# Gated linear attention into a gated layer on one core: late units form queries and decayed states over all partitions and move them, in a new order

## The chip, the cores and the metric

One core of one Trainium2 chip runs the kernel. The metric is device time in microseconds (us) of one execution. Five engines work side by side and wait for each other through semaphores: PE (TensorE, matrix products), DVE (VectorE), ACT (ScalarE), POOL (GpSimd) and SP (SyncE, which here issues nearly all transfers, one after the other in the order of its queue).

## The reference

Inputs are q, k, v and alpha of shape (4, 8, 768, 48), that is 4 sequences, 8 heads, 768 steps, 48 features, and three weight matrices. First a linear attention with a decay for each feature:

```
for t in range(S):
    state = alpha[:, :, t, :, None] * state + einsum('bhd,bhe->bhde', k[:, :, t], v[:, :, t])
    y[:, :, t] = einsum('bhd,bhde->bhe', q[:, :, t], state)
```

Then y, as x of shape (3072, 384), goes through a gated layer with d_ff = 1536:

```
gate = 1 / (1 + exp(-(x @ w_gate)))
out  = (gate * (x @ w_val)) @ w_out
```

The weights come in as 64-bit floats.

## The kernel before

**The layer.** The 3072 tokens are six groups of 512. The 1536 columns of d_ff are twelve pieces of 128, so there are 72 steps (L712 on). A step computes gate and value of one piece for one group: nine matmuls of 512 columns each (L237), three for each of three products, since x and the weights are each split into a high and a low part and high*high, high*low and low*high are added. ACT makes the sigmoid `sg`, DVE multiplies (L727), ACT rounds the product to `hh` (L728), DVE makes the rest `hl` (L729), and nine matmuls (L737) add hh and hl times w_out into three banks `po`. A step is 27 matmuls of 512 columns.

**The weights.** In the first pass over the twelve pieces, each piece is loaded in halves into one of a few `raw` buffers (two of their own, others borrowed from the tiles of weights that are not made yet: `first_w`), and turned into high and low words: a cast of the top bits (ACT, L368, or DVE for the halves in CASTS, L366), a shift-and-or on DVE (L371), a copy to the high part on ACT (L374), and a subtraction to the low part on DVE (L381). For the three halves in SUMS, the low part is written as a negative copy by ACT and added up by a transfer of POOL (L378).

**The attention.** Each group has four pairs of heads, so there are 24 units of one group and one pair, numbered 0 to 23. The two heads of a pair stand on partitions 0 to 47 and 64 to 111. A unit is cut into chunks. Scans along time on DVE make the running decay from the chunk's end, `G` (L409), and from its start, `F` (L413); keys are multiplied by G (`kt`, L417), queries by F. PE makes scores and each chunk's addition to the state; DVE masks the scores into `A` and runs the states through the chunks (`st`), a chain of small operations (L674); the states times the decay `dec` are needed with the queries for the part of the output that comes from earlier chunks. `yt` holds the outputs, and SP moves them into the x tiles of the next group (L462), where heads and partitions are laid out anew.

Units 0 to 5 use chunks of 128. Units 6 to 23 are `late` units with chunks of 64. Their output is one matmul for each head and chunk (L693): the 128 partitions of its operands hold the masked scores and v on one half and the query and the decayed state on the other. For head 0 the query lies on partitions 0 to 63 of `A[:, 0]`, for head 1 on 64 to 127 of `A[:, 1]`. So before, SP loads each half of the query straight into `A` (L624), and DVE multiplies each half by F in place, 64 partitions by 512 (L632, two for each unit); POOL multiplies states by `dec` on each half, 64 by 384, into `vs` (L681, two for each unit).

**The order.** Each operation is handed to a planner (`Plan.add`) with its engine, an estimated duration, a due time and what it reads and writes. The planner places all operations by a model of the engines, and among those that are ready takes the one that is due first. SHIFTS moves the due time of single operations, by their number. Each engine then runs its list in that order. PE's list begins with WARM = 29 products of nothing useful while the first unit is made.

Of the kernel before, what the change touches and what calls it, by code (L numbers as in the profile page):

```python
# [198 lines left out]
def act(n):  # L199
    return 0.01 + n / 1065  # L200
# [40 lines left out]
def chunked(ctx, tc, rows, vc, vh, vg, weights_in, out, const, ident, flags, weights, within):  # L241
# [63 lines left out]
    r_F = ring("F", 2, T, early=[borrow("x1", T)])  # L305
    r_G0, r_dec = ring("G0", 2, EH), ring("dec", 4, EH)
# [42 lines left out]
    def weight_piece(f, key):  # L349
        cuts = (0, DM, 2 * DM, WF) if f == 0 else (0, WF // 2, WF)  # L350
        over = before(f"w{f}") if f >= 6 else []
        for i, (lo, hi) in enumerate(zip(cuts, cuts[1:])):
# [22 lines left out]
            if (f, i) in SUMS:  # L375
                plan.add("scalar", act(n), kk, lambda low=low, word=word: nc.scalar.activation(
                    out=low(), in_=word, func=AF.Copy, scale=-1.0), [rl, ("wh", f, i)], [("w", f, i)])
# [228 lines left out]
    def late(u, g, p, t):  # L606
# [3 lines left out]
        plan.add("sync", (0.475, P * A_Q * 4 / RATE), t["load"], lambda: nc.sync.dma_start(  # L610
            out=tin[:, 0:A_Q], in_=rows[g, p, :, 0:A_Q]), writes=[(inn, m) for m in "ark"])
        kT = tin[:, A_K:A_Q]
# [10 lines left out]
        for j in range(2):  # L623
            plan.add("sync", (0.475, R * T * 4 / RATE), t["more"], lambda j=j: nc.sync.dma_start(  # L624
                out=A[own[j], j], in_=rows[g, p, own[j], A_Q:WIDTH]), writes=[(an, 2 + j)])
        plan.add("sync", (0.475, P * CH * 2 * D * 4 / RATE), after(t["more"], 0.1), lambda: nc.sync.dma_start(
            out=v.rearrange("p c j e -> p (c j e)"), in_=vc[g, p]), writes=[(vn, "v")])
        for j in range(2):
            plan.add("sync", (0.475, R * EH * D * 4 / RATE), after(t["more"], 0.2), lambda j=j: nc.sync.dma_start(
                out=vs[other[j], j].rearrange("p c e -> p (c e)"), in_=vh[g, p, j]), writes=[(vsn, j)])  # L630
        for j in range(2):
            plan.add("vector", 0.61, t["q"], lambda j=j: nc.vector.tensor_tensor(  # L632
                out=A[own[j], j], in0=A[own[j], j], in1=F[own[j]], op=ALU.mult), [fn], [(an, 2 + j)], port=True)
# [209 lines left out]
SUMS = ((3, 0), (5, 1), (9, 0))  # L843
# [171 lines left out]
```

## Time and profile before

| | us |
|---|---|
| median of 3 runs (lowest, highest) | 516.16 (515.01, 516.84) |
| the profiled execution | 515.34 |
| its span on the core | 513.6 |
| PE busy | 503.1 |
| DVE busy | 346.9 |
| ACT busy | 172.3 |
| POOL busy | 95.8 |

The profile is of one execution. Times in it count from the first instruction. Busy time of PE overlaps with itself, since a matmul is shown from its start to the end of its pipeline; what PE really needs for one is read from the distance between two starts. An engine that sits idle and bounds nothing costs nothing. The granted clock is 1.00 (of 2.4 GHz) in the stretches shown below.

### The profile page before, as it was taken

Reading aid. Unit: us, or ns where it says so; the run is one execution under the profiler, and the core shown is the slowest. Engines: PE = TensorE matmul, PEld = TensorE weight load, DVE = VectorE, ACT = ScalarE, POOL = GpSimd, SP = SyncE. Lnnn points to the kernel's source line nnn. Section 1 sums busy time; section 2 is a strip of 40 time slices with the busy share of each in tenths; the row PEclk is TensorE's granted clock in tenths of the full one; section 3 lists DMA queues with packets and bytes.
Section 4 is the critical chain, followed back from the end, with each engine's and each line's share of the span. In section 5 each row is a group of like instructions: output and inputs, shape, how many; then the busy total and the mean of one; then the engine's idle time right before and its main releaser. Section 6 shows DMA issues by size and latency. Waiting matters only on the chain.

```text
span 513.6 us, 10505 instructions
## 1 busy us (share of the span) xinstructions
PE 503.1 (98%) x4223; PEld 428.3 (83%) x4223; DVE 346.9 (68%) x660; ACT 172.3 (34%) x329; POOL 95.8 (19%) x112
## 2 busy tenths in 40 slices
PE   8999999999999999999999999999999999999994
PEld 4878878788888888888888888888888888888884
DVE  7899999999767795669569658568666432222222
ACT  2447665663222133222233323222332222312121
POOL 4450203213302320203113123022021010000000
PEclk9999999999999999999999999999999999999999
DMA  8857985760724553624625625435633000100001
GB/s 313 300 145 226 308 266 177 210 201 11 202 40 121 124 115 74 160 56 124 127 45 129 173 60 131 84 87 131 144 88 73 10 8 17 61 1 0 2 1 66
DMA packets 81111, 59.18 MB, mean 115 GB/s; under 512 B 61984, under 2 KB 67360, under 8 KB 81056
## 3 DMA queue, kind: packets, MB, share of 16 engines
q1 hardware_dynamic: 80624, 57.56, 41.4%
q0 software_dynamic: 432, 0.88, 1.0%
q8 instruction: 34, 0.56, 0.5%
q14 instruction: 21, 0.17, 0.1%
HBM read 45.22 MB, written 8.39 MB: 104 GB/s over the span
## 4 chain that ended last, share of the span: by engine, by line
PE 86%; DVE 10%; DMA 1%; issue 1%; ACT 0%; POOL 0%; DVEq 0%; ACTq 0%; POOLq 0%
PE gv L237 49%; PE po L737 26%; PE gv L693 3%; PE at L645 2%; PE gv L704 1%; DVE w L381 1%; PE at L651 1%; DVE raw L371 1%; DMA in<-in_rows_dram 1%; DVE G L409 1%; DVE first_w L371 1%; DVE F L413 1%; PE at L509 1%; DVE hl L729 1%; DVE A L661 1%
## 5 line engine op out<-in xcount | busy, mean ns | idle before, releaser
L237 PE MATMUL gv<-x,w 128*128 128x512 f32 x1296 | 302.2, 380 | 1.1 <-DVE st L537 0.6
L237 PEld LDWEIGHTS gv<-x,w 128*128 128x128 f32 x1296 | 243.7, 189 | 37.9 <-DVE st L537 1.0
L727 DVE TENSOR_TENSOR gv<-gv,sg 128x512 f32<-128x512 f32 x72 | 50.0, 694 | 118.3 <-PE gv L237 117.9
L737 PE MATMUL po<-hh,w 128*128 128x512 f32 x432 | 109.6, 385 | 0.1
L737 PEld LDWEIGHTS po<-hh,w 128*128 128x128 f32 x432 | 79.7, 189 | 12.3 <-ACT hh L728 0.7
L681 POOL TENSOR_TENSOR vs<-st,dec 64x384 f32<-64x384 f32 x36 | 41.8, 1161 | 250.8 <-PE gv L237 177.0
L728 ACT CAST hh<-gv 128x512 fp32r<-128x512 f32 x72 | 42.3, 588 | 126.0 <-DVE gv L727 120.0
L725 ACT ACTIVATE sg<-gv 128x512 f32<-128x512 f32 x72 | 42.9, 596 | 101.0 <-PE gv L237 99.5
L729 DVE TENSOR_TENSOR hl<-gv,hh 128x512 fp32r<-128x512 f32 x72 | 49.6, 689 | 20.8 <-ACT hh L728 18.6
L737 PE MATMUL po<-hl,w 128*128 128x512 f32 x216 | 60.3, 380 | 0.5 <-DVE hl L729 0.5
L737 PEld LDWEIGHTS po<-hl,w 128*128 128x128 f32 x216 | 40.7, 189 | 7.0 <-DVE hl L729 1.3
L674 DVE SCALAR_TENSOR_TENSOR st<-st,dec,at 128x48 f32<-128x48 f32 x144 | 38.0, 264 | 4.3
L409 DVE TENSOR_TENSOR_SCAN G<-in,d1g 128x512 f32<-128x512 f32 x22 | 33.5, 1523 | 3.2 <-DMA in<-in_rows_dram 3.2
L632 DVE TENSOR_TENSOR A<-A,F 64x512 f32<-64x512 f32 x36 | 32.1, 893 | 2.2 <-DMA A<-in_rows_dram 1.7
L661 DVE TENSOR_TENSOR A<-at,mask 64x256 f32<-64x256 f32 x72 | 30.2, 420 | 3.7 <-PE at L651 3.0
L417 POOL TENSOR_TENSOR in<-in,G 128x512 f32<-128x512 f32 x17 | 23.0, 1353 | 28.5 <-PE gv L430 17.2
L413 DVE TENSOR_TENSOR_SCAN F<-in,d1f 128x512 f32<-128x512 f32 x22 | 27.7, 1258 | 0.5
L423 ACT ACTIVATE F<-F 128x512 f32<-128x512 f32 x23 | 14.5, 632 | 21.5 <-DVE A L632 19.9
L693 PE MATMUL gv<-A,vs 128*48 128x64 f32 x576 | 19.8, 221 | 0.0
L693 PEld LDWEIGHTS gv<-A,vs 128*48 128x48 f32 x576 | 17.1, 123 | 2.1 <-POOL vs L681 0.7
L419 ACT COPY starts<-G 128x8 f32<-128x8 f32 (+1 forms) x23 | 4.7, 203 | 33.1 <-DVE G L409 33.1
L645 PEld LDWEIGHTS at<-A,in 48*64 48x64 f32 x576 | 10.2, 134 | 6.6 <-issue 6.0
(137 smaller groups left out, 330.9 us busy)
## 6 DMA issues: line engine op xcount, KB each, us to landing
in<-in_rows_dram SPq DMA_DIRECT2D x18, 516.5 KB, 4.4
raw<-in_w_dram SPq DMA_DIRECT2D x14, 577.0 KB, 4.1
first_w<-in_w_dram SPq DMA_DIRECT2D x8, 577.0 KB, 4.7
A<-in_rows_dram SPq DMA_DIRECT2D x36, 128.0 KB, 3.3
out_dram<-raw SPq DMA_DIRECT2D x18, 256.0 KB, 2.5
v<-in_vc_dram SPq DMA_DIRECT2D x20, 192.0 KB, 3.0
way<-G SPq DMA_DIRECT2D x14, 256.0 KB, 3.2
kn<-way SPq DMA_DIRECT2D x56, 64.0 KB, 4.2
```

What stands on the lines that cost most here:

```text
L237: nc.tensor.matmul(out=dst, lhsT=lhs(a, i), rhs=rhs(b, i), start=(n == 0 and i == 0), stop=(n == len(todo) - 1 and i == NK - 1))
L409: plan.add("vector", scan(n), t["G"], lambda: nc.vector.tensor_tensor_scan(out=G[:, ::-1], data0=az[:, n:0:-1], data1=d1g[size], initial=0 ...
L413: plan.add("vector", scan(n), after(t["G"], 0.01), lambda: nc.vector.tensor_tensor_scan(out=F, data0=az[:, 0:n], data1=d1f, initial=0.0, o ...
L661: plan.add("vector", 0.43, t["mask"], lambda pa=pa, j=j, i=i: nc.vector.tensor_tensor(out=A[other[j], j].rearrange("p (c i t) -> p i c t", ...
L674: nc.vector.scalar_tensor_tensor(out=st[:, c + 1, :], in0=st[:, c, :], scalar=dec[:, c:c + 1], in1=pas[c % 2][1][:, T // 2 + c // 2 * D:T ...
L681: plan.add("gpsimd", pool_(EH * D), t["sd"], lambda j=j: nc.gpsimd.tensor_tensor(out=vs[own[j], j], in0=st[own[j], 0:EH], in1=dec[own[j]]. ...
L693: nc.tensor.matmul(out=py[R * j:R * j + D, cs], lhsT=vs[r, j, c, :], rhs=A[r, j, cs], start=True, stop=True)
L725: plan.add("scalar", act(T), first(0.3), lambda: nc.scalar.activation(out=sg, in_=got["g"][1][:, 0:T], func=AF.Sigmoid), [got["g"][0]], [sgn])
L727: plan.add("vector", vec(T), first(0.4), lambda: nc.vector.tensor_tensor(out=pv, in0=pv, in1=sg, op=ALU.mult), [sgn], [pvn])
L728: plan.add("scalar", act(T), first(0.45), lambda: nc.scalar.copy(out=hh, in_=pv), [pvn], [hhn])
L729: plan.add("vector", vec(T), first(0.5), lambda: nc.vector.tensor_tensor(out=hl, in0=pv, in1=hh, op=ALU.subtract), [pvn, hhn], [hln])
L737: nc.tensor.matmul(out=pso_now[m][1][:, 0:T], lhsT=weights.part("o", b, f)[:, m * P:(m + 1) * P], rhs=halves(h[a]), start=(f == 0 and i == ...
```

## The change

For the late units four things are different, and the order is new.

- Queries: the whole row of a unit, its query included, is loaded in one transfer into `in`. One operation multiplies the query by F over 128 partitions, on DVE for the units in WHOLE and from unit 10 on, and on POOL for unit 6 alone. Two transfers of SP move each head's half into its place in `A`.
- States: one POOL operation over 128 by 384 writes the decayed states into a new ring of two tiles, `sd`; two transfers of SP move each half into `vs`.
- The tables: QUERIES (early units whose query product is on DVE) gains 2 and 5; KEYS has 8 in the place of 7; SUMS and CASTS name other halves, three and three, where CASTS named five.
- SHIFTS is another table, so that the planner lays out every engine's list anew. A scratch space for transfers that POOL issues is set to 8192.

```diff
+    r_sd = ring("sd", 2, EH, D)
...
-        plan.add("sync", (0.475, P * A_Q * 4 / RATE), t["load"], lambda: nc.sync.dma_start(
-            out=tin[:, 0:A_Q], in_=rows[g, p, :, 0:A_Q]), writes=[(inn, m) for m in "ark"])
-        kT = tin[:, A_K:A_Q]
+        plan.add("sync", (0.475, P * WIDTH * 4 / RATE), t["load"], lambda: nc.sync.dma_start(
+            out=tin, in_=rows[g, p]), writes=[(inn, m) for m in "arkq"])
+        kT, qT = tin[:, A_K:A_Q], tin[:, A_Q:WIDTH]
...
-        for j in range(2):
-            plan.add("sync", (0.475, R * T * 4 / RATE), t["more"], lambda j=j: nc.sync.dma_start(
-                out=A[own[j], j], in_=rows[g, p, own[j], A_Q:WIDTH]), writes=[(an, 2 + j)])
...
+        e = "vector" if u in WHOLE or u >= 2 * NP + 2 else "gpsimd"
+        plan.add(e, vec(T) if e == "vector" else pool_(T), t["q"], lambda: getattr(nc, e).tensor_tensor(
+            out=qT, in0=qT, in1=F, op=ALU.mult), [(inn, "r"), fn], [(inn, "q")], port=True)
         for j in range(2):
-            plan.add("vector", 0.61, t["q"], lambda j=j: nc.vector.tensor_tensor(
-                out=A[own[j], j], in0=A[own[j], j], in1=F[own[j]], op=ALU.mult), [fn], [(an, 2 + j)], port=True)
+            plan.add("sync", (0.475, 2 * R * T * 4 / RATE), after(t["q"], 0.3), lambda j=j: nc.sync.dma_start(
+                out=A[own[j], j], in_=qT[own[j]]), [(inn, "q")], writes=[(an, 2 + j)])
...
+        qn, sd = r_sd.next()
+        plan.add("gpsimd", pool_(EH * D), t["sd"], lambda: nc.gpsimd.tensor_tensor(
+            out=sd, in0=st[:, 0:EH], in1=dec.rearrange("p (c o) -> p c o", o=1).broadcast_to([P, EH, D]), op=ALU.mult), [sn, decn], [qn])
         for j in range(2):
-            plan.add("gpsimd", pool_(EH * D), t["sd"], lambda j=j: nc.gpsimd.tensor_tensor(
-                out=vs[own[j], j], in0=st[own[j], 0:EH], in1=dec[own[j]].rearrange("p (c o) -> p c o", o=1).broadcast_to([R, EH, D]), op=ALU.mult),
-                [sn, decn], [(vsn, 2 + j)])
+            plan.add("sync", (0.475, 2 * R * EH * D * 4 / RATE), after(t["sd"], 0.2), lambda j=j: nc.sync.dma_start(
+                out=vs[own[j], j], in_=sd[own[j]]), [qn], [(vsn, 2 + j)])
...
-SUMS = ((3, 0), (5, 1), (9, 0))
-CASTS = ((3, 0), (4, 0), (5, 0), (8, 0), (9, 1))
-QUERIES = (0, 1, 4)
-KEYS = (0, 1, 3, 4, 6, 7)
+SUMS = ((3, 0), (3, 1), (6, 1))
+CASTS = ((0, 2), (7, 0), (11, 1))
+QUERIES = (0, 1, 2, 4, 5)
+WHOLE = (4, 5, 7, 8, 9)
+KEYS = (0, 1, 3, 4, 6, 8)
...
-    nc = _bacc.Bacc("TRN2", target_bir_lowering=False, num_devices=1)
+    nc = _bacc.Bacc("TRN2", target_bir_lowering=False, num_devices=1, dynamic_dma_scratch_size=8192)
```

In the rows of the order that follow, a name's number is that of the tile, and lines of the new kernel stand a few numbers higher (L409 is L411, L522 is L524, L729 is L733, L363 is L364).

DVE before, at the start, around the masks of unit 2 (`first_x_77`) and the first scan of unit 3 (L409 on `first_w_74`):

```order
L522 TENSOR_TENSOR A_88<-gv_122,mask_104 128x512
L522 TENSOR_TENSOR A_88<-at_119,mask_104 128x512
L537 SCALAR_TENSOR_TENSOR st_110<-st_110,dec_99,at_120 128x48
L522 TENSOR_TENSOR first_x_77<-gv_123,mask_104 128x512
L522 TENSOR_TENSOR first_x_77<-gv_122,mask_104 128x512
L409 SCALAR_TENSOR_TENSOR G_92<-first_w_74,d1g_102 128x512
L371 SCALAR_TENSOR_TENSOR raw_82<-raw_82,top_84 128x384
```

And in the new order:

```order
L499 TENSOR_TENSOR first_w_75<-first_w_75,first_x_77 128x512
L524 TENSOR_TENSOR A_88<-gv_124,mask_106 128x512
L524 TENSOR_TENSOR A_88<-at_121,mask_106 128x512
L372 SCALAR_TENSOR_TENSOR raw_82<-raw_82,top_84 128x384
L539 SCALAR_TENSOR_TENSOR st_112<-st_112,dec_101,at_122 128x48
L411 SCALAR_TENSOR_TENSOR G_92<-first_w_74,d1g_104 128x512
L524 TENSOR_TENSOR first_x_77<-gv_125,mask_106 128x512
L524 TENSOR_TENSOR first_x_77<-gv_124,mask_106 128x512
```

The scan of unit 3 stands ahead of unit 2's masks now, and unit 2's query product (L499) is DVE's.

DVE before, around the last `hl` of the first pass (L729, `hl_118`), with unit 10's scans (L409, L413 on `in_78`) and unit 9's second query half (L632):

```order
L674 SCALAR_TENSOR_TENSOR st_108<-st_108,dec_97,at_120 128x48
L409 SCALAR_TENSOR_TENSOR G_91<-in_78,d1g_103 128x512
L727 TENSOR_TENSOR gv_121<-gv_121,sg_113 128x512
L632 TENSOR_TENSOR A_88<-A_88,F_94 64x512
L411 TENSOR_TENSOR G_95<-G_91,tiny 128x8
L412 RECIPROCAL d1f<-G_95 128x8
L729 TENSOR_TENSOR hl_118<-gv_121,hh_116 128x512
L413 SCALAR_TENSOR_TENSOR F_93<-in_78,d1f 128x512
```

And in the new order, where the last `hl` is `hl_120` and `w_1322` the last piece of weights:

```order
L372 SCALAR_TENSOR_TENSOR raw_83<-raw_83,top_84 128x576
L415 SCALAR_TENSOR_TENSOR F_94<-in_79,d1f 128x512
L733 TENSOR_TENSOR hl_119<-gv_123,hh_117 128x512
L383 TENSOR_TENSOR w_1322<-raw_83,w_1322 128x576
L473 TENSOR_TENSOR x_675<-x_675 128x512
L631 TENSOR_TENSOR in_79<-in_79,F_94 128x512
L414 RECIPROCAL d1f<-G_97 128x8
L415 SCALAR_TENSOR_TENSOR F_93<-in_78,d1f 128x512
L731 TENSOR_TENSOR gv_123<-gv_123,sg_115 128x512
L631 TENSOR_TENSOR in_78<-in_78,F_93 128x512
L733 TENSOR_TENSOR hl_120<-gv_123,hh_118 128x512
```

Unit 10's scan F and its query product stand ahead of the last `hl` now; its scan G and the maximum after it (L411 before) are further up the list. The state chain of unit 8 (L674) is also further up.

SP before, from the loads of the weights' pieces 7 and 8 on (`raw` and `first_w_76` from `in_w_dram`):

```order
L363 DMA raw_82<-in_w_dram 128x2308
L363 DMA raw_83<-in_w_dram 128x2308
L363 DMA first_w_76<-in_w_dram 128x2308
L624 DMA A_87<-in_rows_dram 64x512 x2
L462 DMA x_685<-yt_86 48x512
L629 DMA vs_89<-in_vh_dram 64x384 x2
L363 DMA raw_82<-in_w_dram 128x2308
L462 DMA x_685<-yt_86 16x512
L610 DMA in_79<-in_rows_dram 128x1033
```

And in the new order, from piece 8 on:

```order
L686 DMA vs_89<-sd_95 64x384 x2
L464 DMA x_675<-yt_86 48x512
L364 DMA first_w_76<-in_w_dram 128x2308
L364 DMA raw_82<-in_w_dram 128x2308
L628 DMA vs_89<-in_vh_dram 64x384
L634 DMA A_88<-in_79 64x512 x2
L464 DMA x_675<-yt_86 48x512
L364 DMA raw_83<-in_w_dram 128x2308
L628 DMA vs_89<-in_vh_dram 64x384
L634 DMA A_87<-in_78 64x512 x2
L364 DMA first_w_76<-in_w_dram 128x2308
L464 DMA x_675<-yt_86 16x512
```

Unit 6's states (`vs_89<-sd_95`), unit 7's query (`A_88<-in_79`) and unit 8's (`A_87<-in_78`) stand between the loads now, each with its wait; the loads of queries from memory are gone.

## Rows read from the trace of the kernel before

**Rows 1.** The page, busy us of each engine (share of the span) and instructions.

```profile
PE 503.1 (98%) x4223; PEld 428.3 (83%) x4223; DVE 346.9 (68%) x660; ACT 172.3 (34%) x329; POOL 95.8 (19%) x112
```

**Rows 2.** Stretches: length, busy us of each engine (x instructions), granted clock, DMA.

```profile
30.00:40.00 10.00, 9.09 (x99) 7.13 (x99) 9.96 (x20) 5.31 (x11) 3.83 (x5) 1.00 0.58 170
130.00:400.00 270.00, 270.00 (x2452) 234.14 (x2451) 192.71 (x370) 76.99 (x155) 56.20 (x52) 1.00 0.46 107
```

**Rows 3.** PE's waits: us in total, times, longest; first and last of seven.

```profile
PE at L704 <- POOL ident masks.py:199: 1.6, 1, 1.6
...
PE gv L237 <- DVE w L381: 0.2, 1, 0.2
```

**Rows 4.** The chain, in order of time: start, us, what.

```profile
102.36 1.03 PE gv L693 x32
...
122.27 1.94 PE gv L237 x9
...
124.66 1.78 PE po L737 x7
```

**Rows 5.** PE's groups in 26.4:124.65: xcount, busy us, mean ns, idle before.

```profile
L237 PE MATMUL gv<-x,w 128*128 128x512 f32 x234 | 55.2, 384 | 1.1 <-DVE st L537 0.6 <-DVE x L602 0.2 <-DVE w L381 0.2
L737 PE MATMUL po<-hh,w 128*128 128x512 f32 x68 | 18.6, 389 | 0.1
L737 PE MATMUL po<-hl,w 128*128 128x512 f32 x33 | 9.8, 385 | 0.5 <-DVE hl L729 0.5
```

**Rows 6.** DVE's timeline, 101:126: start, us, what [idle before, releaser].

```profile
101.65 0.69 DVE L729 TENSOR_TENSOR hl<-gv,hh 128x512 fp32r<-128x512 f32 x1 [0.65 <-ACT hh L728]
...
119.70 1.77 DVE L409 TENSOR_TENSOR_SCAN G<-in,d1g 128x512 f32<-128x512 f32 x1
...
122.57 1.23 DVE L411 TENSOR_TENSOR G<-G,tiny 128x8 f32<-128x8 f32 x1
123.84 0.20 DVE L412 RECIPROCAL d1f<-G 128x8 f32<-128x8 f32 x1
123.96 0.64 DVE L729 TENSOR_TENSOR hl<-gv,hh 128x512 fp32r<-128x512 f32 x1
```

**Rows 7.** DVE's groups in 20:126, columns as in rows 5.

```profile
L413 DVE TENSOR_TENSOR_SCAN F<-in,d1f 128x512 f32<-128x512 f32 x7 | 8.5, 1214 | 0.0
...
L632 DVE TENSOR_TENSOR A<-A,F 64x512 f32<-64x512 f32 x8 | 5.5, 682 | 0.1
...
L366 DVE CAST top<-first_w 128x576 f16<-128x576 bf16 x2 | 1.1, 532 | 0.0
...
L440 DVE STREAM_TRANSPOSE G<-in 128x512 f32<-128x512 f32 x1 | 0.7, 711 | 0.1
...
L497 DVE TENSOR_TENSOR in<-in,F 128x512 f32<-128x512 f32 x1 | 0.7, 676 | 0.0
```

**Rows 8.** DVE's timeline, 17:22.

```profile
19.93 1.29 DVE L522 TENSOR_TENSOR first_x<-gv,mask 128x512 f32<-128x512 f32 x2 [1.20 <-PE gv L509]
21.14 1.22 DVE L409 TENSOR_TENSOR_SCAN G<-first_w,d1g 128x512 f32<-128x512 f32 x1
```

**Rows 9.** POOL's timeline, 50:126.

```profile
51.29 1.83 POOL L497 TENSOR_TENSOR in<-in,F 128x512 f32<-128x512 f32 x1 [4.69 <-DVE F L413]
...
119.56 2.53 POOL L681 TENSOR_TENSOR vs<-st,dec 64x384 f32<-64x384 f32 x2 [13.32 <-DVE st L674]
122.17 1.62 POOL L417 TENSOR_TENSOR in<-in,G 128x512 f32<-128x512 f32 x1
```

**Rows 10.** DMA issues: xcount, KB each, median us to landing.

```profile
raw<-in_w_dram SPq DMA_DIRECT2D x14, 577.0 KB, 4.1
...
A<-in_rows_dram SPq DMA_DIRECT2D x36, 128.0 KB, 3.3
```

**Rows 11.** DVE's timeline, 57.3:62.

```profile
58.12 1.22 DVE L413 TENSOR_TENSOR_SCAN F<-in,d1f 128x512 f32<-128x512 f32 x1
```

**Rows 12.** PE's timeline, 68:71.

```profile
69.06 0.69 PE L645 MATMUL at<-A,in 48*64 48x64 f32 x32
```

More of the change, by code (lines that the diff above doesn't have):

```diff
@@ L374, in weight_piece @@
             plan.add("scalar", act(n), kk, lambda word=word, high=high: nc.scalar.copy(out=high(), in_=word), [rl], [("wh", f, i), *over])
-            if (f, i) in SUMS:
-                plan.add("scalar", act(n), kk, lambda low=low, word=word: nc.scalar.activation(
-                    out=low(), in_=word, func=AF.Copy, scale=-1.0), [rl, ("wh", f, i)], [("w", f, i)])
+            summed = (f, i) in SUMS
+            plan.add(*(("scalar", act(n)) if summed else ("vector", 0.0)), kk, (lambda low=low, word=word: nc.scalar.activation(
+                out=low(), in_=word, func=AF.Copy, scale=-1.0)) if summed else (lambda: None), [rl, ("wh", f, i)], [("w", f, i)])
+            if summed:
                 plan.add("gpsimd", (0.9, P * n * 8 / RATE), kk, lambda low=low, word=word: nc.gpsimd.dma_start(
@@ L840, in chunked @@
         plan.issue()
-SUMS = ((3, 0), (5, 1), (9, 0))
-CASTS = ((3, 0), (4, 0), (5, 0), (8, 0), (9, 1))
-QUERIES = (0, 1, 4)
-KEYS = (0, 1, 3, 4, 6, 7)
-SHIFTS = ((5, -2), (12, -4), (51, 8), (52, 5), (54, 8), (71, 6), (82, 2), (85, 1), (93, -8), (126, 3), (143, 4), (160, 9), (170, 1), (177, 5), (179, 2), (187, 10), (219, -1), (222, 21), (237, -1), (282, 12), (290, -5), (302, 3), (324, 3), (325, -4), (338, 4), (343, -8), (347, -13), (348, -1), (355, 2), (360, 2), (370, 2), (373, 6), (374, 9), (376, 6), (388, 2), (402, 2), (403, 4), (416, -4), (418, 6), (440, -5), (464, -10), (468, 34), (480, -3), (493, 5), (494, 4), (503, -2), (519, 16), (565, -3), (573, -2), (583, 6), (588, -2), (598, -1), (601, 7), (622, -4), (658, 3), (699, 2), (803, 12), (829, 8), (860, 2), (863, -1))
+SUMS = ((3, 0), (3, 1), (6, 1))
[3 more added lines that the diff above has]
+KEYS = (0, 1, 3, 4, 6, 8)
+SHIFTS = ((5, -4), (55, 31), (64, 7), (67, -19), (68, 42), (82, 27), (92, 38), (96, -7), (101, -35), (103, -10), (109, -40), (110, -17), (115, 44), (123, 13), (124, 5), (126, 31), (131, 36), (158, -45), (161, 523), (166, 51), (169, 301), (173, 97), (191, 87), (193, 58), (202, 39), (213, -82), (215, 69), (219, -2), (244, -75), (245, 53), (269, -15), (271, -35), (283, 59), (287, 66), (294, 21), (306, 730), (312, 47), (323, 16), (325, -158), (335, 32), (338, 61), (345, -3), (346, -15), (347, -14), (348, 19), (351, 123), (357, 275), (360, 541), (361, 921), (369, -5), (377, -31), (382, 199), (384, -24), (392, 142), (400, 30), (401, 9), (421, -125), (433, 122), (450, 220), (451, 451), (452, 33), (457, 74), (462, -48), (464, 6), (471, 141), (472, 5), (476, 270), (487, -9), (499, 62), (501, -70), (504, -78), (505, -64), (513, 29), (523, 159), (528, 113), (533, -33), (535, 76), (536, -12), (540, 128), (541, 2), (544, 66), (547, 21), (567, 33), (579, -27), (581, 82), (598, -26), (601, 71), (604, 172), (605, 196), (611, 17), (621, -110), (629, -45), (632, -45), (643, 95), (656, -43), (682, -23), (684, -18))
 WARM = 29
```

## The prediction

> **What bounds the kernel now.** I read the page first, then the stretches, then PE's waits, then DVE's timeline where those waits lie. PE is busy in 98% of the span [rows 1], so a change of this kind can only win what PE loses. The stretches say where it loses: from 130 us on PE is busy without a gap while DVE works 193 of 270 us; in 30:40 it is DVE that is full, 9.96 of 10 us, and PE that has a hole of 0.9 [rows 2]. PE's waits are seven, 3.8 us together; the largest, 1.6 us, is the start of the kernel, and the other six are for DVE [rows 3]. Gaps understate the loss, since a matmul that starts late hides part of it: nine of 512 columns take 1.94 us in a row, 0.2156 us each [rows 4], though each is shown as 0.38 us long [rows 5]. From the first weight matmul at 26.4 us to 124.65 us PE issued 234 + 68 + 33 = 335 of those [rows 5], 72.2 us of issue. The attention matmuls of the same 98.25 us, each bunch from its start to the next one's (as 1.03 us for the outputs of a late unit, L693 [rows 4]; there are some thirty bunches), make 18.6 us. So 98.25 - 72.2 - 18.6 = 7.4 us are lost there. That is the most that the change can win apart from the 26 us of the start.
>
> The end of this stretch is set by DVE: the last `hl` of the first pass over the weights starts at 123.96 us, lasts 0.64 us, and is read by a matmul that starts at 124.66 [rows 4, 6]. Behind it PE has 382.5 us of gapless work and a tail, which no edit touches. So I ask: when does DVE make its last `hl` of the first pass, and how much of PE's work stands behind it then?
>
> **The change part by part.** Durations are means of DVE's rows in 20:126 [rows 7].
>
> Term 1, DVE's own work ahead of that `hl`. Removed: eight half-height query products (units 6 to 9, 8 x 0.682 = 5.5 us) and three 576-column casts of weights (3 x 0.53 = 1.6). Added: four full-height products (units 7 to 10; unit 6 goes to POOL). No row shows a full-height product of a late unit; the nearest is L497, 0.676, so the other 64 partitions are free: 4 x 0.676 = 2.7. Two query products of units 2 and 5 come from POOL: 1.35. One 384-column cast: at most 0.53, I take 0.4. Unit 10 is drawn ahead of the last `hl` with its F scan (1.21), transposition (0.71) and a product of 8 columns (under 0.2). Removed 7.1, added 6.5: -0.5 us. Without unit 10, whose four instructions are 2.7 us, it would be -3.3; both are kept for the range.
>
> Term 2, a stall that is filled. At 18.7 us DVE stood 1.20 us for the scores of unit 2, and then ran masks and a scan of 1.22 us [rows 8]. The order now has that scan ahead of the masks. The scores are as late as before, but the wait is covered: -1.2 us, as long as PE's scores keep their place, which they do. Bounds: -1.2 to 0.
>
> Term 3, POOL in DVE's way. Between the last weight words and the last `hl`, two DVE instructions are stretched: the scan at 119.70 took 1.77 us instead of 1.22, and the 8-column maximum L411 at 122.57 took 1.23 us where the reciprocal of the same 8 columns takes 0.20 [rows 6]. Both ran beside POOL products of SBUF operands, 119.56 and 122.17 [rows 9]. That is 0.55 + 1.03 = 1.6 us. In the new order unit 10's scan and maximum are earlier and unit 8's decayed states, now one POOL product, are long done. But POOL still multiplies unit 10's keys, now ahead of the last weights, so I put 1.0 back; the halved decay products of units 6 and 7 give perhaps 0.2, my estimate. Term 3: -0.8, bounds -1.9 (nothing is stretched again) to +1.0 (unit 9's keys too meet DVE, and unit 6's query adds to it, 1.83 us on POOL as L497 is there [rows 9]). The Trainium skill (SBUF — State Buffer, section "SBUF: two separate sides") says that the pair of ports which DVE and GpSimd share is an exclusive lock, held for a whole instruction. By that rule the two POOL entries would have stopped two-operand work on DVE for all of their 4.15 us, and with unit 10's keys (1.62) put back the term would be -2.5 and the sum -3.0. The trace does not bear this out to the full: DVE went on with other work beside them and lost the 1.6 above.
>
> Term 4, work left behind. Ahead of its last `hl` PE now issues 225 + 103 = 328 of the 512-column matmuls instead of 335 by the order (nine fewer of the second pass, two more of the first); the attention matmuls ahead of it are the same number. Seven are left for later: 7 x 0.2156 = +1.5 us.
>
> Term 5, DVE's wait of 0.65 us for ACT at 101.65 [rows 6]. ACT gets two more casts and DVE's order there is another; I take half of it as gone: -0.3, bounds -0.65 to +0.65.
>
> What I cost at nothing. The transfers: no row shows a move of a query or of states; the nearest are loads of 128 KB, which land in 3.3 us [rows 10]; I take that for both. They lengthen two chains of each unit. Unit 6: F is done at 59.3 us in the old order [rows 11] and its scores start at 69.06 [rows 12]; POOL 1.8, two issues and 3.3 come to about 6.3, so 3 us of cover are left. Later units have their query made about 1.5 steps (8.7 us) ahead of the scores and their states over two steps ahead of the outputs, and DVE has slack from 130 us on [rows 2]. If the cover were gone, each late unit would cost PE the rest of one transfer. The loads of unit rows carry the same bytes as before, in one instead of three. POOL's halved work is off the path later, and the smaller scratch concerns three POOL transfers only.
>
> Sum: -0.5 - 1.2 - 0.8 + 1.5 - 0.3 = -1.3 us. The profiled execution took 515.34 us (span 513.6), 0.8 under the median of 516.16; taken off the median: 514.9, rounded to the side of the larger cover in terms 1 and 3, 514.8.
>
> **The rivals.** About 0.3%, 1.55 us, can be told from no change.
>
> Full relief: early unit 10 is only taken where DVE would wait, so that term 1 counts -3.3, and term 3 -1.1. Then -3.3 - 1.2 - 1.1 + 1.5 - 0.3 = -4.4, or 511.8. For it: DVE is full to 120 us [rows 2]. Against: PE must then find its other inputs sooner too, and 7.4 us is all there is.
>
> No gain: the last `hl` comes earlier but PE meets a wait elsewhere (the last weight words stand 0.7 us of DVE's queue later in this order than before, counted as in term 1), so only the small waits shift: 516.2, give or take 0.8.
>
> Slower: SP. It issues in order, and now two products per unit stand in its queue with their waits. In 80 to 110 us the load of a weight piece stands behind unit 7's query, the move of unit 6's `yt`, or unit 8's query; the load lands after 4.1 us [rows 10], then ACT casts it, then DVE needs it. Between the release of a buffer and its next use lie about 7 us of DVE's queue; 4.1 go to the load, up to 1.5 to the move of `yt` ahead of it, and the cast takes most of the rest, so that three loads (both halves of piece 9, the first of 11) have about half a us to spare each. If each comes 2 us later, DVE stands still three times for 1.5 us; it decides as soon as the sum is over the 1.3 us above: 4.5 - 1.3, net +3, or 519. For it: buffers are only three. Against: the loads mostly wait for their buffer, not for their turn. The Trainium skill (DMA: Bandwidth & Descriptors, section "Anatomy of one DMA") says that a semaphore wait happens on the issuing sequencer before dispatch, so nothing behind it starts; this is that mechanism.
>
> **How the numbers follow.** My forecast 0.50, own range 513.2 to 516.2: a little under half of it is faster by over 0.3%. Full relief 0.23, no gain 0.14, slower 0.13. Faster: 0.24 + 0.23 = 0.47; within 0.3%: 0.26 + 0.14 = 0.40; slower 0.13. The range leaves out a tenth on either side: 510.8 (most of full relief) to 518.0 (half of the slower case).
>
> **What would show it.** Right: no wait of DVE near 19 us; the last `hl` of the first pass at about 121 to 122.5 us; POOL's decay products 18 and not 36; PE without gaps after 130 us. Wrong: weight words on DVE that wait for ACT casts or loads between 85 and 112 us (the slower rival); a PE wait for a query or states moved by transfer; a last `hl` under 120 us (full relief).

## The result and the profile after

The changed kernel took 520.71 us (median of six runs, 518.68 to 522.07), the kernel before 516.29 beside it (six runs, 514.83 to 517.01). The ratio is 1.0087 [1.0060, 1.0113]: slower by 0.9%, or 4.4 us, where I had forecast 1.4 us faster. The profiled execution took 520.46 us, with a span of 518.7.

The page's first part, busy us of each engine in the changed kernel (before: [rows 1]):

```profile
PE 502.8 (97%) x4223; PEld 427.5 (82%) x4223; DVE 321.2 (62%) x641; ACT 174.7 (34%) x331; POOL 70.2 (14%) x93
```

DVE and POOL are each relieved by 26 us, as the change says, and PE's work is the same. So the 5.1 us of span are waits. Busy time by stretch tells where (length, busy us of PE, PEld, DVE, ACT, POOL with their counts, granted clock, DMA share, GB/s). The kernel before:

```profile
20.00:126.00 106.00, 103.47 (x953) 85.82 (x948) 103.52 (x192) 61.00 (x111) 26.55 (x29) 1.00 0.65 196
126.00:140.00 14.00, 14.00 (x153) 12.12 (x152) 10.36 (x21) 4.24 (x8) 4.00 (x4) 1.00 0.71 176
```

The changed kernel:

```profile
20.00:126.00 106.00, 100.28 (x940) 83.08 (x935) 97.14 (x186) 62.64 (x113) 19.09 (x23) 1.00 0.72 217
126.00:140.00 14.00, 12.93 (x141) 10.34 (x141) 9.52 (x21) 4.24 (x8) 2.33 (x3) 1.00 0.66 161
```

PE is busy for 3.2 us less ahead of 126 us and 1.1 us less behind it; from 140 to 400 us it has no gap in either kernel. Of the 6.4 us by which DVE is less busy in the first stretch nothing reached PE. The waits show what took its place. PE's largest from 20 us on (us in total, times, longest):

```profile
PE po L741 <- ACT hh L732: 3.1, 4, 1.8
PE gv L237 <- ACT sg L729: 1.3, 2, 0.7
PE gv L237 <- ACT yt L457: 1.2, 1, 1.2
```

And DVE's in 20:127, where the kernel before had three waits of 1.2, 0.7 and 0.3 us (the first two are in [rows 6, 8]):

```profile
DVE raw L372 <- ACT top L369: 5.0, 4, 2.0
DVE G L411 <- DMA in<-in_rows_dram: 1.0, 1, 1.0
DVE first_w L372 <- ACT first_w L369: 0.6, 1, 0.6
DVE w L383 <- ACT w L375: 0.3, 1, 0.3
```

PE used to wait for DVE [rows 3]; now it waits for ACT, and DVE does too. ACT's timeline shows why (start, us, what, idle before and its releaser), around 65 and 95 us:

```profile
64.67 0.83 ACT L369 CAST top<-raw 128x576 f16<-128x576 bf16 x1 [1.50 <-DMA raw<-in_w_dram]
65.37 0.57 ACT L457 COPY yt<-gv 128x512 f32<-128x512 f32 x1
...
94.18 0.83 ACT L369 CAST top<-raw 128x576 f16<-128x576 bf16 x1 [1.79 <-DMA raw<-in_w_dram]
94.88 0.57 ACT L436 COPY kn<-gv 128x512 f32<-128x512 f32 x1
95.35 0.59 ACT L732 CAST hh<-gv 128x512 fp32r<-128x512 f32 x1
```

PE at the same two places:

```profile
66.00 0.70 PE L237 MATMUL gv<-x,w 128*128 128x512 f32 x2 [1.22 <-ACT yt L457]
...
95.99 0.48 PE L741 MATMUL po<-hh,w 128*128 128x512 f32 x1 [1.76 <-ACT hh L732]
```

The reader is to see a queue here. A cast of weights waits for its load, and what PE needs next (`yt`, which frees a bank; `hh`) stands behind it in ACT's list and waits too, though its own input is long there: the outputs that `yt` copies were made by 61.7 us, the product that `hh` rounds by 92.3. Late loads alone are not the difference. From 20 to 127 us ACT waited 6.3 us for loads of weights, and about as long, 6.0, in the kernel before, where PE has no wait for ACT at all. The third place is the start of the second pass. DVE, 130 to 135 us:

```profile
130.40 1.73 DVE L663 TENSOR_TENSOR A<-at,mask 64x256 f32<-64x256 f32 x4 [2.45 <-PE at L653]
132.14 2.37 DVE L676 SCALAR_TENSOR_TENSOR st<-st,dec,at 128x48 f32<-128x48 f32 x8
134.42 0.69 DVE L731 TENSOR_TENSOR gv<-gv,sg 128x512 f32<-128x512 f32 x1
```

PE there:

```profile
130.30 2.21 PE L237 MATMUL gv<-x,w 128*128 128x512 f32 x9
133.25 2.21 PE L237 MATMUL gv<-x,w 128*128 128x512 f32 x9 [0.75 <-ACT sg L729]
135.79 1.56 PE L741 MATMUL po<-hh,w 128*128 128x512 f32 x6 [0.33 <-ACT hh L732]
```

The gate of the first piece (130.30) comes behind the gate of the next piece and unit 10's scores, and its product waits on DVE behind four masks and eight states.

Gaps understate what is lost, as before. So I counted for each kernel, at every group of PE's list, its start less the issue time of all that stands ahead of it (0.2156 us for a 512-column matmul [rows 4], the others by their own rows). These are worked out from one profiled execution each and are good to about half a us, since the small matmuls have no one price; the kernels from the third row on are the experiments below:

| lost on PE by, us | 27 | 47 | 62 | 97 | 126.6 | 146 | end |
|---|---|---|---|---|---|---|---|
| before | 5.0 | 8.1 | 8.3 | 11.5 | 12.6 | 12.7 | 16.0 |
| changed | 5.1 | 7.3 | 8.2 | 13.9 | 15.5 | 17.5 | 20.5 |
| both_undone | 5.3 | 7.5 | 8.4 | 12.3 | 15.3 | 17.4 | 20.3 |
| sum_on_vector | 5.2 | 7.7 | 8.2 | 11.5 | 13.0 | 15.0 | 18.0 |
| mended2 | 5.2 | 7.4 | 8.0 | 9.6 | 10.2 | 15.9 | 18.9 |
| mended3 | 5.1 | 7.3 | 8.0 | 10.8 | 11.6 | 13.0 | 16.0 |
| mended3_old_ops | 5.2 | 7.4 | 8.0 | 11.9 | 15.3 | 15.7 | 18.6 |

The change loses 2.5 us more than before from 62 to 97 us, 0.5 to 126.6, and 1.9 at the start of the second pass; at the end it is 4.5.

### The profile page after: what moved, and what is told of

It is laid out like the page before. It is cut to its first block, busy times and chain, and to the rows that moved or that the text cites. A ratio compares the mean times of both kernels' runs of the same rounds, so it can differ in the third digit from the quotient of the medians.

```text
span 518.7 us, 10513 instructions
## 1 busy us (share of the span) xinstructions
PE 502.8 (97%) x4223; PEld 427.5 (82%) x4223; DVE 321.2 (62%) x641; ACT 174.7 (34%) x331; POOL 70.2 (14%) x93
## 2 busy tenths in 40 slices
DMA packets 83991, 67.44 MB, mean 130 GB/s; under 512 B 62560, under 2 KB 70240, under 8 KB 83936
## 4 chain that ended last, share of the span: by engine, by line
PE 75%; DVE 15%; DMA 5%; issue 2%; ACT 1%; SPq 0%; DVEq 0%; ACTq 0%
PE gv L237 45%; PE po L741 24%; DMA first_w<-in_w_dram 3%; PE gv L697 3%; PE at L647 2%; DVE G L411 2%; DVE w L383 2%; DVE raw L372 2%; DVE first_w L372 1%; DMA raw<-in_w_dram 1%; DVE st L676 1%; DVE F L415 1%; PE at L653 1%; DVE gv L731 1%; DVE A L663 1%
## 5 line engine op out<-in xcount | busy, mean ns | idle before, releaser
L729 ACT ACTIVATE sg<-gv 128x512 f32<-128x512 f32 x72 | 43.0, 597 | 128.6 <-PE gv L237 128.6
L733 DVE TENSOR_TENSOR hl<-gv,hh 128x512 fp32r<-128x512 f32 x72 | 49.3, 685 | 21.6 <-ACT hh L732 19.7
L741 PE MATMUL po<-hl,w 128*128 128x512 f32 x216 | 61.8, 382 | 0.2 <-DVE hl L733 0.2
L683 POOL TENSOR_TENSOR sd<-st,dec 128x384 f32<-128x384 f32 x18 | 15.5, 862 | 270.0 <-DVE st L676 224.8
L411 DVE TENSOR_TENSOR_SCAN G<-in,d1g 128x512 f32<-128x512 f32 x22 | 30.4, 1381 | 9.4 <-DMA in<-in_rows_dram 9.4
L415 DVE TENSOR_TENSOR_SCAN F<-in,d1f 128x512 f32<-128x512 f32 x22 | 28.9, 1316 | 0.1
L457 ACT COPY yt<-gv 128x512 f32<-128x512 f32 x20 | 11.7, 585 | 14.3 <-PE gv L697 14.3
L473 DVE TENSOR_TENSOR x<-x 128x512 fp32r<-128x512 f32 x15 | 10.3, 688 | 7.5 <-ACT x L471 7.5
```

Source lines behind the costliest of these rows:

```text
L411: plan.add("vector", scan(n), t["G"], lambda: nc.vector.tensor_tensor_scan(out=G[:, ::-1], data0=az[:, n:0:-1], data1=d1g[size], initial=0 ...
L415: plan.add("vector", scan(n), after(t["G"], 0.01), lambda: nc.vector.tensor_tensor_scan(out=F, data0=az[:, 0:n], data1=d1f, initial=0.0, o ...
L729: plan.add("scalar", act(T), first(0.3), lambda: nc.scalar.activation(out=sg, in_=got["g"][1][:, 0:T], func=AF.Sigmoid), [got["g"][0]], [sgn])
L733: plan.add("vector", vec(T), first(0.5), lambda: nc.vector.tensor_tensor(out=hl, in0=pv, in1=hh, op=ALU.subtract), [pvn, hhn], [hln])
L741: nc.tensor.matmul(out=pso_now[m][1][:, 0:T], lhsT=weights.part("o", b, f)[:, m * P:(m + 1) * P], rhs=halves(h[a]), start=(f == 0 and i == ...
```

## The experiments

Two theories stood against each other. M: the new operations cost the time, by the moves that stand in SP's queue and by their traffic, so that weights land late. O: the operations are harmless or good, and the order that was found anew is the worse one. All kernels were timed in five rounds against the kernel before; intervals are of 95%.

**Operations and order taken apart.** A part of the plan keeps its place in every engine's list when only what it issues is changed. So old operations can stand in the new order and new ones in the old.

both_undone and states_undone, the core of the edit for the states (both_undone does the like for the queries):

```
-   plan.add("gpsimd", ..., nc.gpsimd.tensor_tensor(out=sd, in0=st[:, 0:EH], ...
+   plan.add("gpsimd", ..., [nc.gpsimd.tensor_tensor(out=vs[own[j], j], in0=st[own[j], 0:EH], ...) for j in range(2)]
-   plan.add("sync", ..., nc.sync.dma_start(out=vs[own[j], j], in_=sd[own[j]])
+   plan.add("sync", ..., lambda: None)
```

> The changed kernel in its own new order of instructions on every engine, but with the old operations put back in place: the query halves are loaded from DRAM into A by two loads and multiplied on VectorE where the one product stood, the two state products on GpSimd write vs where the one product stood, and no SBUF-to-SBUF move is left (two more A buffers, since in this order the queries come earlier). Theory M (the moves and their waits in SP's in-order queue, and their traffic, make the weight pieces land late): the late loads go away, 515 to 517 us. Theory O (the order that was found for the new kernel, with its casts, sums and shifts, is the worse one whichever way the operations are done): it stays at 520 to 521 us.

Measured: 519.66 us, 1.0083 [1.0068, 1.0097]. Without one of the new operations, the new order is as slow as the changed kernel. But it is not the same loss. By the table both_undone loses 3.9 us from 62 to 97 us, where the changed kernel loses 5.7, and 3.0 to 126.6, where that loses 1.6; ACT's waits for loads at 64 and 94 us are gone, which is what M had named as its sign. The old operations, longer on DVE and POOL, lose elsewhere what the late loads no longer cost. So equal times do not clear the moves by themselves; mended3 below does.

> The changed kernel with the states times decay alone put back: two products of 64 partitions on GpSimd straight into vs in the place of the one, without their 36 moves; the queries stay as changed. Theory M: half of the moves are gone, so a good part of the 4.4 us: 517 to 519 us. Theory O: 520 to 521 us, or a little more, since GpSimd works longer (about 26 us of it in all).

Measured: 520.83 us, 1.0098 [1.0079, 1.0116]. Half of the moves gone, nothing won.

moves_on_pool issues all 72 moves by `nc.gpsimd.dma_start`:

> The changed kernel with all 72 moves issued from GpSimd's queue in place of SP's, in the same places of the order; the traffic is the same. Theory M in its form of the queue (weight loads stand behind moves that wait for their product): 516 to 518 us. Theory M in its form of the traffic (the moves' bytes share the DMA engines with the weights), and theory O: 520 to 521 us or more, as GpSimd takes about 1 us for each issue.

Measured: 519.56 us, 1.0095 [1.0072, 1.0117]. In its profiled execution the wait at 94 us was gone, but its six runs lay between 517.9 and 522.2 us, no better than the changed kernel's. So to take the moves off SP's queue wins nothing as it stands; what POOL's issuing of them costs instead is not told apart.

The other half of the cross is the old order with the new operations. In the first of these two kernels a late unit's whole row could be loaded while an early unit's outputs still had to read their query in that buffer, so those outputs are computed with another unit's query:

> The kernel before in its own old order, with the new operations put in place: whole query rows are loaded, one product of 128 partitions stands where the second of the two stood, and its two moves follow right there; the same for the states. Theory M: slower than before by about what the change cost, 519 to 521 us. Theory O: 515 to 516.5 us, as before or a little faster, since VectorE works less.

Measured: 528.61 us, 1.0253 [1.0229, 1.0277]; since it computes something else it is not counted for O or M. The second loads the query by itself, when its place in `A` is free:

> The kernel before in its own old order of instructions, with the new operations put where the first of each pair of old ones stood: the query rows are loaded whole at the place of the first A load, the one product of 128 partitions and its two moves stand at the place of the first half product, and the same for the states. Theory O (the new order is the cause, the operations are harmless): 515 to 517 us. Theory M (the operations and their moves cost the time): 519 us or more; of that a wait of TensorE for A<-in or vs<-sd would show the move's own 2 to 3 us behind the product, for which the old order has no room.

Measured: 523.88 us, 1.0203 [1.0161, 1.0246]; four of its six runs lay between 523.3 and 524.1 us, two at 528.6 and 529.7. PE's two largest waits from 20 us on:

```profile
PE gv L705 <- DMA vs<-sd: 5.1, 2, 3.4
PE at L652 <- DMA A<-in: 1.4, 1, 1.4
```

Here M has a point: in a list made for operations without moves there is no room for a move behind the product, and PE waits for it. In those places the new operations don't pay, and a new order was needed. In the changed kernel PE has no wait for a move; there it is only that the new order loses time elsewhere.

**The start of the second pass.** MOVED names parts of the plan that are put ahead of others, with everything else as in the changed kernel:

```
+MOVED = ((643, 655),)        # gate of the second pass's first piece, ahead of the next piece's gate
```

> The changed kernel with one group of nine matmuls put earlier on TensorE alone: the gate of the second pass's first weight piece stands ahead of the gate of the next piece and of unit 10's scores and additions (it stood behind them, at 130.30 us), so VectorE has its product out before the four masks and eight states that held it from 132.14 to 134.42 us. Theory O: the 1.7 us that the new order loses between 130 and 137 us go away, about 519 us where the changed kernel has 520.7 (ratio to before 1.005 to 1.006). Theory M: nothing changes, 520.7 us (1.0087).

Measured: 522.84 us, 1.0146 [1.0123, 1.0168]. The edit made it worse, and the trace says why. PE and DVE of gate_first:

```profile
137.35 2.93 PE L746 MATMUL po<-hh,w 128*128 128x512 f32 x6 [3.28 <-ACT hh L737]
```

```profile
131.96 1.73 DVE L668 TENSOR_TENSOR A<-at,mask 64x256 f32<-64x256 f32 x4 [4.39 <-PE at L658]
133.70 2.37 DVE L681 SCALAR_TENSOR_TENSOR st<-st,dec,at 128x48 f32<-128x48 f32 x8
135.98 0.69 DVE L736 TENSOR_TENSOR gv<-gv,sg 128x512 f32<-128x512 f32 x1
```

I had moved PE's group alone. On DVE the product still stood behind the masks, and the masks now came 1.6 us later because PE's scores did. DVE stood idle until 131.96 us, though ACT had made `sg`, the product's last input, by 129.7, where the idle time ahead of ACT's next instruction begins:

```profile
136.71 0.58 ACT L737 CAST hh<-gv 128x512 fp32r<-128x512 f32 x1 [7.01 <-DVE gv L736]
```

> As gate_first, and the product of gate and value of the piece whose po matmuls waited 0.87 us at 117.46 us stands ahead of a transpose and a shift on VectorE, and its hh ahead of two copies on ScalarE. Theory O: another 1.0 us less, about 518 us (ratio 1.003 to 1.004). Theory M: 520.7 us (1.0087).

Measured: 523.05 us, 1.0136 [1.0114, 1.0159]; the same loss hides what the added edit does.

> gate_first with what it lacked: not TensorE's gate group alone goes ahead of unit 10's scores, but also its product on VectorE goes ahead of unit 10's four masks and eight states (in gate_first the product stood behind them in the in-order queue, and TensorE waited 3.28 us for hh). Theory O (the places of a few instructions in the new order): the loss between 127 and 137 us falls from 1.8 us in the changed kernel to about 0.1, so 1.7 us less than the changed kernel, about 519 us where it has 520.7 (ratio to before 1.005 to 1.006). Theory M (the operations and their moves): 520.7 us (1.0087).

Measured: 522.05 us, 1.0139 [1.0121, 1.0157]. PE no longer waits for `hh`, but 2.64 us for `hl`, which stands behind a scan on DVE that waits for rows. My expectation failed a second time, for the same reason one instruction further on.

**The load that comes late.** The row of POOL's timeline that issues the accumulating transfer for piece 3, its landing among the DMA issues (xcount, KB, us to landing), and SP's next load into that buffer, in the changed kernel:

```profile
48.75 0.86 POOL L380 DMA_DIRECT2D w<-raw  x1 [4.59 <-DVE d1f L414]
```

```profile
w<-raw POOLq DMA_DIRECT2D x1, 288.0 KB, 9.3
```

```profile
58.10 0.33 SPq L364 DMA_DIRECT2D raw<-in_w_dram  x1
```

The transfer holds its `raw` from 48.75 to 58.08 us, and the next load starts at 58.10: it is the load for which ACT waits at 64.67. Before, SUMS named (5, 1) and (9, 0) where it now names (3, 1) and (6, 1). gate_product_sum and sum_on_vector make that low part on DVE (the later runs name such halves in ON_VECTOR):

```
-   plan.add("gpsimd", ..., nc.gpsimd.dma_start(out=low().bitcast(F32), in_=word, accum_op=ALU.add), ...)
+   plan.add("gpsimd", ..., nc.vector.tensor_tensor(out=low(), in0=word, in1=high(), op=ALU.subtract), ...)   # for (3, 1)
```

> As gate_and_product, and the low part of piece 3's second half is made by a VectorE subtraction in place of the accumulating transfer, which held its raw buffer from 48.75 to 58.08 us, so that the next load into it starts at once. If the late loads between 58 and 77 us come from the buffer that is held: 0.5 to 1.4 us less again, 516.5 to 517.5 us (ratio 1.001 to 1.003). If they come from the moves' traffic: no change against gate_and_product.

Measured: 520.94 us, 1.0107 [1.0086, 1.0128], against 1.0136 [1.0114, 1.0159] for gate_and_product; the intervals overlap.

> The changed kernel with one edit: the low part of piece 3's second half by a VectorE subtraction in place of the accumulating transfer that held its raw buffer from 48.75 to 58.08 us. If the buffer that it holds makes the weight loads behind it late (gate_product_sum had 2.1 us less than gate_and_product): 518 to 519 us (ratio 1.004 to 1.006). If the moves' traffic makes them late: 520.7 us (1.0087).

Measured: 517.24 us, 1.0032 [1.0017, 1.0047]: more than half of the loss from one edit. ACT of sum_on_vector at the place of the wait of 1.50 us:

```profile
63.19 0.98 ACT L369 CAST top<-raw 128x576 f16<-128x576 bf16 x1
64.03 0.62 ACT L458 COPY yt<-gv 128x512 f32<-128x512 f32 x1
```

The load comes just in time, and `yt` with it. At the other place ACT's wait of 1.79 us has shrunk too, though on SP the moves of a query stand ahead of that load as before:

```profile
91.50 0.97 ACT L369 CAST top<-raw 128x576 f16<-128x576 bf16 x1 [0.37 <-DMA raw<-in_w_dram]
```

The edit also spares ACT the negative copy (0.69 us at 47.76). That is not what won: ACT stands idle behind it in either kernel, and its next instruction starts at 50.20 us in the one and 50.24 in the other.

No load waits on SP for the two other such transfers, so I took them out as well:

> The changed kernel with all three accumulating transfers replaced by VectorE subtractions (sum_on_vector replaced one). If such a transfer costs by the buffer that it holds and the load behind it: at or below sum_on_vector, 515.5 to 517 us (ratio 1.000 to 1.003). If VectorE's added 1.3 us count in full: 1.004 to 1.006.

Measured: 518.23 us, 1.0058 [1.0046, 1.0070]; its six runs lay within 0.4 us of each other. The expectation that it be at or below sum_on_vector was wrong, and the time lies where the added work of DVE counts in full: the likely price of each is its subtraction (0.74 us in the changed kernel).

> sum_on_vector's order and subtraction with the old operations put back as in both_undone (no moves). If the accumulating transfer costs by itself, with or without moves: 2 to 3 us less than both_undone, ratio 1.003 to 1.005. If it costs only because VectorE's relief is there to take the subtraction, or because the moves stretch it: as both_undone, 1.008, and then the new operations are worth what sum_on_vector (1.0032) has less.

Measured: 519.10 us, 1.0072 [1.0060, 1.0084]. With the old operations the same edit wins 0.1% (both_undone 1.0083; the intervals overlap), with the new ones 0.55%. That fits a DVE which must be relieved before the late load is what PE waits for; no run shows it by itself.

**Both mends.**

> The changed kernel with its operations and moves as they are and three local edits of its order: gate_ahead, the product and hh of gate_and_product, and the subtraction of sum_on_vector. By gate_product_sum's trace (12.6 us lost on TensorE by 126 us, then 5 us that gate_ahead's edit takes away) theory O gives 515 to 517 us (ratio 0.999 to 1.003). Theory M: 518 us or more (1.006 and up).

Measured: 518.49 us, 1.0062 [1.0042, 1.0081], above the range expected of it: the wait for `hl` of gate_ahead is there too (2.30 us), and with it the kernel is slower than with the transfer alone replaced (sum_on_vector, 1.0032).

> mended's order with the old operations put back in their places as in both_undone (no moves, half products on VectorE, state halves on GpSimd). What the operations themselves are worth once the order is mended: if they are worth nothing, the same as mended within 0.2%; if the moves cost, 1 to 3 us less than mended; if the relief of VectorE is worth something, 1 us or more above it.

Measured: 520.64 us, 1.0093 [1.0078, 1.0108].

> mended with one more place: the low half hl of the same piece also goes ahead of unit 10's masks (in mended it stood behind a scan that waited for its rows until 135.35 us, and TensorE waited 2.30 us for the bank that hl frees). If the loss at the start of the second pass is a matter of places in the in-order queues: 2.5 us less than mended, 515 to 516.5 us (ratio 0.999 to 1.002). If the second pass loses as much whatever stands where: as mended, 1.006.

Measured: 518.97 us, 1.0077 [1.0058, 1.0095]. The wait moved on once more. DVE and PE of mended2:

```profile
134.12 1.22 DVE L417 TENSOR_TENSOR_SCAN G<-in,d1g 128x512 f32<-128x512 f32 x1 [1.96 <-DMA in<-in_rows_dram]
135.26 0.67 DVE L737 TENSOR_TENSOR gv<-gv,sg 128x512 f32<-128x512 f32 x1
```

```profile
137.60 3.28 PE L242 MATMUL gv<-x,w 128*128 128x512 f32 x9 [2.34 <-DVE hl L739]
```

Now the next piece's product stands behind unit 11's scan, whose rows land at 134 us.

> mended2 with no accumulating transfer: both mends together. If they add up: 514 to 516 us (ratio 0.997 to 1.001), level with the kernel before or a little faster. If they take the same slack: as the better of mended2 and no_sums.

Measured: 520.04 us, 1.0078 [1.0059, 1.0096]: not added up, as in no_sums.

The last one puts that product, `hh` and `hl` ahead of the scan too:

```
+MOVED = ((643, 655), (645, 668), (646, 668), (647, 668), (648, 668),   # gate, sg, product, hh, hl of the first piece
+         (658, 751), (659, 751), (660, 751),                           # product, hh, hl of the next one
+         (589, 684), (590, 294))                                       # product and hh at 115 us
+ON_VECTOR = ((3, 1),)
```

> mended2 with the next piece's product, hh and hl also ahead of unit 11's first scan on VectorE, which in mended2 waited 1.96 us for its rows (landed at 134.03 us) with that product queued behind it, so that TensorE waited 2.34 us at 137.60 us. If the loss at the start of the second pass is a matter of what stands behind a waiting instruction in VectorE's queue: 2.5 to 4.5 us less than mended2, 514.5 to 516.5 us (ratio 0.999 to 1.003). If it only moves on to the next instruction again: 1.006 or more.

Measured: 515.31 us (twelve runs, 514.54 to 516.53), 1.0003 [0.9994, 1.0012]. Its stretches:

```profile
20.00:126.00 106.00, 103.44 (x953) 85.38 (x948) 98.91 (x188) 63.58 (x114) 18.42 (x22) 1.00 0.70 216
126.00:140.00 14.00, 14.00 (x152) 11.86 (x151) 10.89 (x23) 3.65 (x8) 2.33 (x3) 1.00 0.70 174
```

PE is as busy as before the change in both, with the changed kernel's operations, moves and traffic. One transfer replaced and ten parts of the plan put earlier in three lists give back the whole 0.84%. The transfer was tried by itself (0.55%), the ten parts only together.

> mended3 (1.0003 to before) with the old operations in the places of the new ones, as in both_undone: 18 pairs of half products on VectorE, 18 pairs of half state products on GpSimd, no moves. What the new operations are worth in an order without the two losses: by the two pairs measured so far (sum_on_vector 1.0032 against sum_old_ops 1.0072, mended 1.0062 against mended_old_ops 1.0093) 1.6 to 2.1 us, so 517 to 517.5 us (ratio 1.003 to 1.005). If they are worth nothing: 515.3 us (1.000).

Measured: 517.48 us, 1.0035 [1.0022, 1.0049]. In one and the same order the new operations are worth 0.3%, some 1.7 us; the two other pairs (sum_on_vector with sum_old_ops, mended with mended_old_ops) show 0.4 and 0.3%. In the order as it came with the change the pair shows nothing (1.0087, and 1.0083 with the old operations). So in none of four orders do the new operations and their moves cost time, and in three they save some, in two of these clear of the intervals; all four orders were laid out for them. No version beat the kernel before beyond its interval.

## Why the prediction was wrong

**The step that failed** is the one between term 1 and the sum: that what DVE no longer does comes out as an earlier last `hl`, with nothing lost behind it ("Behind it PE has 382.5 us of gapless work and a tail, which no edit touches"). DVE was relieved and then waited. Its last `hl` of the first pass starts at 124.56 us (123.96 before [rows 6]), where I had put 121 to 122.5, and PE reads it at 126.20 us instead of 124.66 [rows 4]:

```profile
124.56 0.69 DVE L733 TENSOR_TENSOR hl<-gv,hh 128x512 fp32r<-128x512 f32 x1
```

```profile
126.20 0.38 PE L741 MATMUL po<-hl,w 128*128 128x512 f32 x1
```

The start of the second pass, which I took for untouched, lost 1.9 us. I had priced the instructions that the order moves, and not what the new neighbours of an instruction make it wait for. The operations on which I had spent most of the working don't decide: without them the time is the same (both_undone), and mended3 has them all, with their moves, and loses nothing.

**Term 1** (-0.5): the direction holds, DVE's busy time in 20:126 fell by 6.4 us, in part because work was pushed behind 126 us; in mended3, where PE does as much by then as before, it is 4.6 us less, with a subtraction more. A full-height product of a late unit, which no row of before showed, takes what I took from L497 [rows 7] (683 ns, the mean of four).

**Term 2** (-1.2): right on DVE. The stall at 18.7 us [rows 8] is filled, and the scan runs with no idle time ahead of it:

```profile
19.04 0.54 DVE L372 SCALAR_TENSOR_TENSOR raw<-raw,top 128x384 uint32<-128x384 uint32 x1
19.51 0.25 DVE L539 SCALAR_TENSOR_TENSOR st<-st,dec,at 128x48 f32<-128x48 f32 x1
19.68 1.35 DVE L411 TENSOR_TENSOR_SCAN G<-first_w,d1g 128x512 f32<-128x512 f32 x1
```

By 47 us PE had 0.8 us of it (7.3 against 8.1 lost); by 62 us hardly any is left (8.2 against 8.3).

**Term 3** (-0.8): the relief is there. POOL's work in 20:126 fell from 26.55 to 19.09 us, and the scan of G that stood at 119.70 and took 1.77 us [rows 6] now takes 1.22:

```profile
112.35 1.22 DVE L411 TENSOR_TENSOR_SCAN G<-in,d1g 128x512 f32<-128x512 f32 x1
```

It did not reach PE, which takes the last `hl` 0.95 us after DVE has made it, without a wait. The 4.15 us of POOL that I held against DVE there are too many by the trace itself: the second state half took 1.63 us, and such halves take 0.83 where no scan of DVE runs beside them (last section), so about 0.8 us of it was POOL being held up.

**Term 4** (+1.5): nothing in the runs contradicts it; the last `hl` is 1.5 us later and PE has that much less to its credit, so 3 us were lost by then.

**Term 5** (-0.3): wrong in sign and the largest error of a single term. DVE's waits for ACT rose from 1.0 us to 5.9. I saw that ACT gets two more casts and that DVE's order is another, and did not follow ACT's queue.

**Transfers at nothing:** right for PE, which waits for no move in the changed kernel; old_order_new_ops2 is the price when the cover is gone, 6.5 us of waits. But the loads I took as unchanged land later. Rows of the changed kernel, median us to landing in the last column (before: 4.1 for `raw` and 3.3 for a query half [rows 10], 4.7 for `first_w`):

```profile
raw<-in_w_dram SPq DMA_DIRECT2D x14, 577.0 KB, 5.1
first_w<-in_w_dram SPq DMA_DIRECT2D x8, 577.0 KB, 6.5
A<-in SPq DMA_DIRECT2D x36, 128.0 KB, 2.5
```

The 2.5 us of a query's move are a median of the whole run; the eight in 20:127 took 4.1.

Part of that may be the moves' bytes (67.44 MB in all against 59.18), part that loads are issued closer together; no run separates the two. mended3 has all of it and loses nothing, so it can be borne.

**The rivals.** The slower one named the time (519) and one true half: weight pieces that land late, and engines that stand still for them. Its sign, weight words on DVE that wait for casts between 85 and 112 us, is there (0.58 us at 90.78, 1.19 at 95.05). Its mechanism did not decide. The trace does show one load behind moves on SP, the one for which ACT waits at 94.18:

```profile
85.49 1.19 SPq L634 DMA_DIRECT2D A<-in  x2
86.77 0.55 SPq L464 DMA_DIRECT2D x<-yt  x1
87.41 0.53 SPq L364 DMA_DIRECT2D raw<-in_w_dram  x1
```

DVE's last read of its buffer starts at 85.44 us and takes 0.70, so the load comes some 1.3 us late. But in sum_on_vector the same transfers stand ahead of it and ACT waits 0.37 us; by my matching of the records with the lists, 17 of the 21 weight loads from 20 to 127 us start within 0.15 us of their buffer's release (14 of 21 before); and with every move taken off SP the time stayed at 1.0095. The rule of the Trainium skill that I cited there (DMA: Bandwidth & Descriptors, section "Anatomy of one DMA") agrees with SP's waits in the changed kernel: at one move of states SP stood 5.0 us. It speaks of transfers alone; what decided were waits in ACT's and DVE's lists. "No gain" had the right shape, PE meeting a wait elsewhere, with a price of nothing.

**What stays open:** the runs of the changed kernel spread over 3.4 us, those of before over 2.2 and those of mended3 over 2.0. The late loads may come out differently from run to run, and with one profile for each kernel the share of each place is that of one execution. Which table (SUMS, CASTS, QUERIES, KEYS or SHIFTS) the other 0.5 us ahead of 126 us come from was not tried apart from SUMS. Nor was it tried whether such edits would make the kernel before faster too.

## What to carry to other kernels

A change that brings its own new order is two changes: put the old operations into the new order and the new ones into the old before arguing about either, and compare where the kernels lose as well as how much: the same time can be another loss. When an engine is relieved, read for each consumer on the critical engine what stands directly ahead of its producer in the producer's own list, and whether that can wait; a cast behind a late load or a scan behind late rows passes its whole wait on. Moving one instruction forward on one engine alone can make it worse: its product, copy and release on the other engines have to move with it.

## What the runs showed of the hardware

An accumulating transfer from SBUF into SBUF, 288 KB issued by POOL, landed after 3.8 us (median of two) or 9.3 us. During the latter (48.75 to 58.08 us) the DMA engines' busy share was 1.00 and 2.75 MB moved. The load into its source buffer was issued 0.02 us after it landed.

A state product on POOL took as long over 64 partitions as over 128. The median of the halves in the kernel before is 831 ns (shortest, median, longest):

```profile
L681 POOL TENSOR_TENSOR vs<-st,dec x36: 823/831/1845, 82.8 to 412.8; 64x384 f32<-64x384 f32 x36
```

Of the whole ones in the changed kernel 16 of 18 took 827 to 832 ns:

```profile
L683 POOL TENSOR_TENSOR sd<-st,dec 128x384 f32<-128x384 f32 x18 | 15.5, 862 | 270.0 <-DVE st L676 224.8
```

The halves' mean of 1161 ns is no price of their own. Thirteen of them, each the second of its pair, started while DVE's scan of G ran and took 1.63 to 1.85 us. So one operation for two saves 26 us (41.8 to 15.5) and not half.
